# One x tile loaded ahead of the weights, its transpose halved, and one K product moved, in the QKV stage of a fused attention and feed-forward kernel

## The chip, the cores and the metric

The kernel runs on one core of a Trainium2 chip. The metric is the device time of one execution in microseconds (us). The span, from the first to the last instruction in the trace, comes out 2 us shorter. A few executions are in a slow state (over 1.5% above the fastest); they enter no ratio. The short names of the engines are PE (TensorE, matmuls), DVE (VectorE), ACT (ScalarE), POOL (GpSimd) and SP (SyncE, which issues most loads).

## The reference, cut to what matters

```python
def reference(A_x, A_wqkv, A_wo, B_x, B_w_gate, B_w_up, B_w_down):
    ...
    x = A_x                                  # 1 x 2048 x 1024, bf16
    xn = _layernorm(x, axis=-1)
    s = _A_ref(xn, A_wqkv, A_wo)             # linear attention: K and V of all tokens are summed first
    g = _silu(_B_ref(xn, B_w_gate, B_w_up, B_w_down))
    return x + s * g
```

Only the first 45 us of the program are changed. In them, 16 tiles of 128 tokens are normalised and transposed, and are multiplied with the K and V columns of `wqkv`. Those columns form four chunks of 512, and chunks 0 and 1 are K. The products of each tile are then summed into a state (`kvz`).

## The kernel before

The loads in program order. SP issues nearly all of them on its one queue; ACT issues half of x tile 0:

```python
        def load_x(i):
            if i == 0 and D % 2 == 0:
                h = D // 2
                x_loads[i] = nc.sync.dma_start(out=x_ap(i)[:, 0:h], in_=x2[0:P, 0:h])
                nc.scalar.dma_start(out=x_ap(i)[:, h:D], in_=x2[0:P, h:D])
                return
            x_loads[i] = nc.sync.dma_start(out=x_ap(i), in_=x2[i * P:(i + 1) * P, :])
        # ... (load_wkv(c) loads chunk c of the K and V weights, 1 MB)
        load_x(0)
        load_wkv(0, halves=2 if DC % 2 == 0 else 1)
        nx = 1
        for c in range(1, NCH):
            if nx < NT:
                load_x(nx)
                nx += 1
            load_wkv(c)
        for i in range(nx, NT):
            load_x(i)
        for wt, wv in ((wq_sb, wqkv_v), (wo_sb, wo_v)):
            for c in range(NCC):
                nc.sync.dma_start(out=wt[:, :, c * CW:(c + 1) * CW], in_=wv[:, :, c * CW:(c + 1) * CW])
```

The steps are `emit_stats` and `emit_rstd` (layer norm statistics), `emit_N` (normalise, on DVE), `emit_TR` (eight PE transposes into PSUM, then a copy to `xnT`), `emit_Bmm(i, c)` (product of tile i with chunk c, eight matmuls), `emit_Bev(i, c)` (its evacuation by ACT and DVE) and `emit_C(i)` (accumulation of tile i into `kvz`). Each engine runs its own instructions in the order written here:

```python
        emit_stats(0); emit_rstd_act(0); emit_N(0); emit_TR(0)      # (one call per line in the source)
        emit_stats(1); emit_rstd_act(1); emit_N(1)
        emit_Bmm(0, 0)
        emit_TR(1)
        ln_pre(2, nc.vector)          # statistics and rstd of tile 2, all on DVE
        emit_Bev(0, 0)
        emit_Bmm(0, 1)
        emit_N(2)
        emit_Bmm(1, 0)
        # ...
```

## Time and profile before

| | before |
|---|---|
| first three executions | 767.11, 766.46, 768.77 us |
| span of the profiled execution | 767.3 us (that execution took 769.27 us) |
| PE busy | 754.1 us (98%) |
| PE's longest wait | 2.35 us, for the rows of tile 1 |
| half-clock stretch | 3.41 us, from 12.22 us |

The page of before: span, busy time with instruction counts, and the chain that ended last by engine.

```profile
span 767.3 us, 10482 instructions
PE 754.1 (98%) x3717; PEld 349.6 (46%) x3717; DVE 551.5 (72%) x1076; ACT 345.8 (45%) x473; POOL 287.4 (37%) x413
PE 92%; DVE 4%; ACT 1%; DMA 1%; issue 1%; SPq 0%; ACTq 0%; DVEq 0%
```

PE is the limit, so the gaps in its timeline are what can be won. The timeline of before, PE alone; columns are start, duration, engine, line, operation, count, and in brackets the idle time before it and what ended it.

```profile
6.19 0.72 PE L470 MATMUL tr_ps<-ident,xn 128*128 128x128 bf16 x8 [0.24 <-DVE xn L443]
7.11 1.04 PE L486 MATMUL kv_ps<-wkv_sb,xnT 128*128 128x512 bf16 x4 [0.20 <-DVE xnT L473]
8.34 1.02 PE L486 MATMUL kv_ps<-wkv_sb,xnT 128*128 128x512 bf16 x4 [0.19 <-DMA wkv_sb<-in_A_wqkv_dram]
11.71 0.62 PE L470 MATMUL tr_ps<-ident,xn 128*128 128x128 bf16 x8 [2.35 <-DVE xn L443]
12.17 10.48 PE L486 MATMUL kv_ps<-wkv_sb,xnT 128*128 128x512 bf16 x40
```

PE finishes the first product at 9.36 and idles until 11.71. The chain of waits says for what; columns are start, duration and piece.

```profile
2.21 6.79 DMA xp<-in_A_x_dram
...
9.02 1.29 DVE stats L405 x2
...
11.11 0.56 DVE xn L443
...
11.71 0.62 PE tr_ps L470 x8
```

The load of x tile 1, issued at 2.21, lands at 9.00, and 2.71 us of statistics and normalising follow. The view of DMA issues, narrowed to 2.7 to 2.9 us, shows the next load in the queue, chunk 1; the last number is the time to landing.

```profile
wkv_sb<-in_A_wqkv_dram SPq DMA_DIRECT2D x1, 1024.0 KB, 9.2
```

Issued at 2.75, it lands at 11.98, only 0.19 us before PE uses it. Last, the windows view of before: busy time of each engine in a stretch, then granted clock, DMA busy share and GB/s.

```profile
5.00:6.00 1.00, 0.95 (x4) 0.17 (x2) 0.54 (x3) 0.29 (x1) 0.00 (x0) 1.00 0.84 267
6.00:7.00 1.00, 0.72 (x8) 0.45 (x8) 0.83 (x4) 0.00 (x0) 0.00 (x0) 1.00 0.93 293
8.80:12.22 3.42, 1.07 (x12) 0.57 (x11) 2.20 (x5) 1.61 (x3) 0.00 (x0) 1.00 1.08 376
12.34:15.76 3.42, 3.42 (x9) 1.22 (x8) 3.11 (x11) 0.94 (x2) 0.00 (x0) 0.52 1.09 356
```

The third line is the stretch that holds the gap, with PE busy 1.07 of 3.42 us. In the fourth the clock is half (0.52): nine matmuls in 3.42 us.

### The profile page before, as it was taken

How to read it: one execution, taken by the hardware profiler on the slowest of the kernel's cores; microseconds unless marked ns; L12 is line 12 of the kernel's file. 1: busy time of each engine (PE TensorE's matmuls, PEld its weight loads, DVE VectorE, ACT ScalarE, POOL GpSimd, SP SyncE). 2: the span in 40 equal slices, each digit the busy share in tenths (PEclk: the TensorE clock that was granted, in tenths of full speed). 3: DMA queues.
4: the chain of work that ended last, by engine and by line, in shares of the span. 5: the costliest groups of instructions: out<-in, count | busy, mean ns of one | idle time of the engine just before them, and what ended most of it. 6: DMA issues, size and time to landing. Idle time of an engine off the chain costs nothing.

```text
span 767.3 us, 10482 instructions
## 1 busy us (share of the span) xinstructions
PE 754.1 (98%) x3717; PEld 349.6 (46%) x3717; DVE 551.5 (72%) x1076; ACT 345.8 (45%) x473; POOL 287.4 (37%) x413
## 2 busy tenths in 40 slices
PE   7999999999999999999999999999999999999996
PEld 3544444444444444444444444444444444444443
DVE  6788557997666588878889885358676776787335
ACT  3545667788853566566447411132323223201111
POOL 0477499959685255858656000110000000200000
PEclk9999999999999999999999999999999999999999
DMA  9945868769889769898888227399654444530923
GB/s 308 352 95 114 229 221 274 248 222 259 237 304 262 256 228 312 283 333 298 308 309 290 89 81 262 113 356 334 229 185 167 165 169 175 187 114 23 296 73 117
DMA packets 105396, 170.29 MB, mean 222 GB/s; under 512 B 34688, under 2 KB 82176, under 8 KB 94720
## 3 DMA queue, kind: packets, MB, share of 16 engines
q1 hardware_dynamic: 94960, 121.00, 50.3%
q0 software_dynamic: 7936, 44.31, 15.0%
q10 hardware_dynamic: 2448, 4.33, 1.6%
q8 instruction: 29, 0.48, 0.3%
q14 instruction: 23, 0.19, 0.1%
HBM read 111.67 MB, written 50.59 MB: 211 GB/s over the span
## 4 chain that ended last, share of the span: by engine, by line
PE 92%; DVE 4%; ACT 1%; DMA 1%; issue 1%; SPq 0%; ACTq 0%; DVEq 0%
PE zw L725 25%; PE kv_ps L486 14%; PE dzw L910 13%; PE xb L725 12%; PE s_ps L659 7%; PE yb L725 6%; PE dx L910 6%; PE q_ps L170 4%; PE dy L910 3%; PE kvz L508 1%; DMA xp<-in_A_x_dram 1%; DVE o_blk L640 1%; PE nd_ps L632 1%; DVE pqT L141 1%; DVE pqT L153 0%
## 5 line engine op out<-in xcount | busy, mean ns | idle before, releaser
L725 PEld LDWEIGHTS <-w_sb 128*128 128x128 f16 (+1 forms) x1568 | 152.2, 98 | 184.3 <-issue 1.7
L725 PE MATMUL xb<-xnT,w_sb 128*128 128x512 bf16 x448 | 115.0, 379 | 1.1 <-ACT sg L800 1.1
L486 PE MATMUL kv_ps<-wkv_sb,xnT 128*128 128x512 bf16 x512 | 115.5, 383 | 0.4 <-DVE xnT L473 0.2
L725 PE MATMUL zw<-xnT,w_sb 128*128 128x512 bf16 x448 | 105.8, 379 | 0.0
L725 PE MATMUL zw<-S,w_sb 128*128 128x512 f16 x448 | 105.8, 379 | 0.0
L280 POOL TENSOR_TENSOR w_sb<-w_sb 128x512 f16<-128x512 bf16 x42 | 48.9, 1165 | 96.7 <-DVE w_sb L268 36.3
L247 ACT ACTIVATE w_sb<-w_sb 128x2048 bf16<-128x2048 bf16 x42 | 79.9, 1902 | 9.1 <-DMA w_sb<-in_B_w_up_dram 7.1
L910 PE MATMUL dx<-w_sb,hT 128*128 128x512 bf16 x224 | 82.8, 379 | 0.0
L486 PEld LDWEIGHTS <-xnT 128*128 128x128 bf16 x512 | 49.0, 98 | 57.2 <-issue 2.4
L910 PEld LDWEIGHTS <-hT 128*128 128x128 bf16 (+1 forms) x448 | 43.8, 98 | 52.9
L910 PE MATMUL dzw<-w_sb,hT 128*128 128x512 f16 (+1 forms) x224 | 64.4, 379 | 0.0
L170 PE MATMUL q_ps<-xnT,wq_sb 128*128 128x512 bf16 x256 | 58.2, 379 | 0.0
L753 DVE SCALAR_TENSOR_TENSOR s<-yb,rc_all,s 128x512 f32<-128x512 f32 x42 | 31.5, 749 | 37.0 <-ACT s L752 37.0
L659 PE MATMUL s_ps<-wo_sb,oT 128*128 128x512 bf16 x256 | 57.8, 379 | 0.0
L725 PE MATMUL yb<-S,w_sb 128*128 128x512 f16 x224 | 57.4, 379 | 0.0
L801 ACT ACTIVATE sg<-cg 128x1024 bf16<-128x1024 f32 x28 | 29.6, 1057 | 56.6 <-DVE cg L794 56.6
L794 DVE SCALAR_TENSOR_TENSOR cg<-zw,rc_all,s 128x1024 f32<-128x1024 f32 x28 | 35.9, 1283 | 25.4 <-PE zw L725 14.0
L850 POOL TENSOR_TENSOR hs<-hT 128x512 f16<-128x512 bf16 x2 | 2.5, 1258 | 132.6 <-ACT sg L801 132.6
L281 POOL TENSOR_TENSOR w_sb<-w_sb 128x512 f16<-128x512 bf16 x42 | 50.1, 1193 | 3.3
L283 POOL TENSOR_TENSOR w_sb<-w_sb 128x512 f16<-128x512 bf16 x42 | 50.8, 1210 | 0.0
L282 POOL TENSOR_TENSOR w_sb<-w_sb 128x512 f16<-128x512 bf16 x42 | 49.8, 1186 | 0.0
L884 POOL DMA_DIRECT2D out_dram<-io x16 | 8.7, 542 | 101.9 <-DVE io L883 101.6
(148 smaller groups left out, 1099.3 us busy)
## 6 DMA issues: line engine op xcount, KB each, us to landing
w_sb<-pk_g SPq DMA_DIRECT2D x27, 1024.0 KB, 6.0
pk_g<-w_sb POOLq DMA_DIRECT2D x14, 1024.0 KB, 5.4
pk_u<-w_sb POOLq DMA_DIRECT2D x14, 1024.0 KB, 6.4
w_sb<-wd SPq DMA_DIRECT2D x14, 1024.0 KB, 5.0
w_sb<-pk_u SPq DMA_DIRECT2D x14, 1024.0 KB, 4.9
w_sb<-wd SPq DMA_DIRECT2D x14, 768.0 KB, 5.8
w_sb<-in_B_w_gate_dram SPq DMA_DIRECT2D x14, 512.0 KB, 5.3
w_sb<-in_B_w_down_dram SPq DMA_DIRECT2D x28, 256.0 KB, 4.5
```

Of the source, the lines that this page charges most:

```text
L170: nc.tensor.matmul(q_ps[:], lhsT=wq_sb[:, dc, g * P:(g + 1) * P], rhs=xn_ap(dc, btok), start=(dc == 0), stop=(dc == DC - 1))
L247: nc.scalar.activation(out=junk, in_=raw_view(key, t), func=ACT.Square, accum_out=asum[:])
L280: nc.gpsimd.tensor_tensor(out=T1, in0=b12, in1=b11, op=ALU.subtract)
L281: nc.gpsimd.tensor_tensor(out=T2, in0=b22, in1=T1, op=ALU.subtract)
L282: nc.gpsimd.tensor_tensor(out=T3, in0=b22, in1=b12, op=ALU.subtract)
L283: nc.gpsimd.tensor_tensor(out=T4, in0=b21, in1=T2, op=ALU.subtract)
L486: mm = nc.tensor.matmul(kv_ps[:], lhsT=xn_ap(dc, tok), rhs=wkv_sb[:, dc, c * CW:(c + 1) * CW], start=(dc == 0), stop=(dc == DC - 1))
L659: mm = nc.tensor.matmul(s_ps[:], lhsT=oT[:, c, ttok], rhs=wo_sb[:, c, cc * CW:(cc + 1) * CW], start=(c == 0), stop=(c == G - 1))
L725: mm = nc.tensor.matmul(out, lhsT=lhs(k), rhs=rhs(k), start=(first and k == 0), stop=(k == HK - 1), skip_group_check=True)
L753: nc.vector.scalar_tensor_tensor(out=s2[:], in0=y_[:], scalar=rc, in1=s1[:], op0=ALU.mult, op1=ALU.add)
L794: nc.vector.scalar_tensor_tensor(out=d12, in0=zw[:], scalar=rc, in1=s2[:, None, :].to_broadcast([P, 2, TB]), op0=ALU.mult, op1=ALU.add)
L910: nc.tensor.matmul(out, lhsT=lhs, rhs=rhs, start=first, stop=lastk, skip_group_check=True)
```

## The change

The intent: start x tile 1 right away on the ACT queue instead of behind 1 MB of weights; transpose it in two halves that are copied by two engines (for this, tile 0's copies move from DVE to ACT); and transpose tile 2 and do its first K product earlier, so that PE has work while weights are on their way.

```diff
@@ load_x
+            if i == 1:
+                x_loads[i] = nc.scalar.dma_start(out=x_ap(i), in_=x2[i * P:(i + 1) * P, :])
+                return
@@ order of the loads
         load_x(0)
+        load_x(1)
         load_wkv(0, halves=2 if DC % 2 == 0 else 1)
-        nx = 1
+        nx = 2
         for c in range(1, NCH):
+            load_wkv(c)
             if nx < NT:
                 load_x(nx)
                 nx += 1
-            load_wkv(c)
@@ emit_N
-            if i == 0:
+            if i < 2:
@@ emit_TR
-            nh = 2 if i == 0 else 1
+            nh = 2 if i < 2 else 1
 ...
-                if i < 2:
+                if i == 1 and hh == 0:
                     nc.vector.tensor_copy(out=dst, in_=tr_ps[:])
                 else:
                     nc.scalar.copy(out=dst, in_=tr_ps[:])
@@ order of the stage
         emit_Bmm(0, 2)
+        emit_TR(2)
         emit_Bev(1, 1)
 ...
         ln_pre(4)
-        emit_TR(2)
+        emit_Bmm(2, 0)
         emit_Bmm(0, 3)
 ...
-                emit_Bmm(i, c)
+                if (i, c) != (2, 0):
+                    emit_Bmm(i, c)
```

## The prediction

> **What bounds the kernel now.** The tensor engine (PE). The page gives it 98% of the 767.3 us span, and PE matmuls fill 92% of the chain that ended last. By the table of waits all its waits come to about 7 us, and the largest, 2.4 us, is the one this change aims at: the timeline shows PE finishing the first K product at 9.36, idle until 11.71, when tile 1's normalised rows arrive (chain of waits: x tile 1 issued 2.21, landed 9.00, statistics, rstd, normalise, transpose). After 12.17 PE is gap-free until about 131 us, so whatever is gained or lost near 12 to 30 us should reach the end of the kernel unchanged. In the stretch 12.3 to 15.8 the granted clock was 0.52 (matmul starts 0.43 us apart instead of 0.22), costing about 1.7 us more. The Trainium skill, "TensorE: Matmul & The Clock Gate", Part 1, describes that: a free-running 3.4 us window with too little PE work halves the clock for the next one. The trace agrees: one half-clock stretch of 3.41 us, after a window with PE busy 1.06 of 3.41 us.
>
> **What the change does.** x tile 1 goes to the ACT queue, beside weight chunk 0 instead of behind it. The skill, "DMA: Bandwidth & Descriptors", section "Issuing engines are not separate DMA queues", says queues interleave on the same 16 engines, so this reorders bytes and adds no bandwidth. Estimate from the windows view (about 0.35 MB per us): x1 lands near 5.5; the second half of weight chunk 0 slips by 0.26 MB / 0.36 = 0.7 us, from 8.3 to 9.0. Statistics of tile 1 then follow tile 0 directly (6.5), normalised rows at about 9.3. The first K product ends near 10.1 (0.7 later), transposes of tile 1 follow at once.
>
> **Why most of the 2.4 us isn't won.** The next product in PE order needs weight chunk 1. The DMA view shows it issued at 2.75 and landing 9.2 us later: 11.95, only 0.2 us before PE used it. The bytes ahead of it (x0, x1, chunks 0 and 1) are unchanged, so it still lands near 11.9. The wait changes its name, from x1 to weight chunk 1, and PE gains 0.2 to 0.3 us there.
>
> **Clock.** PE work in the window before 12 us rises from 31% to about 50 to 55%, as the late half of the first product, the transposes and the wait are spread more evenly. If that keeps the full clock, up to 1.7 us is regained, but not all: at full clock the PE meets VectorE's chain for tile 2 (x2 lands 12.7; rstd by small operations until 17.2; first K evacuation 18.4; normalise 18.9), which frees PSUM and feeds transpose 2. I count 0.5 to 0.8 us of new waits.
>
> **The other parts.** Both copies of tile 0's transpose move to ScalarE (1.02 us for 1024 columns there, 0.69 on VectorE): 0.1 to 0.2 us later start, hidden by the chunk-0 wait. Transpose 2 earlier puts its ScalarE copy (1.02 us) before the evacuation of K product (1,1), whose bank product (2,0) needs: 0.4 to 0.6 us wait. Moving (2,0) adds no work.
>
> **Sum.** With the clock kept: 1.2 to 1.5 us faster than a half-clock run; with half clock again: 0.3 faster to 0.3 slower. Predicted 766.2 us, range 764.6 to 768.0; faster by over 2%: 0.005, within 2%: 0.99, slower: 0.005.
>
> **Right if:** x1 lands before 6.5; PE waits 1 us or more for weight chunk 1, ending at 11.6 to 12.0; transposes of tile 1 end before 11; the span changes by less than 2 us. **Wrong if:** weight chunk 1 lands before 11 (gain 2 to 3 us), or the reordered ScalarE work stalls PE by over 1 us near 20 to 24 us.

## More of the kernel before

Tiles 0 to 3 are transposed on PE. From tile 4 on, `emit_N` ends with a DMA transpose on the SP queue:

```python
            if i >= NPE:              # NPE = 4
                xn_tiles.pop(i)
                nc.sync.dma_start_transpose(out=xn_ap(slice(0, DC), slice(i * P, (i + 1) * P)), in_=xn[:])
```

## The result, and the profile after

| | before | after |
|---|---|---|
| median of four | 767.8 us | 765.94 us |
| lowest and highest | 766.46, 768.77 | 765.63, 766.43 |
| span of the profiled execution | 767.3 us | 764.2 us |

The ratio is 0.9978, with a 95% interval of 0.9959 to 0.9996, so "same" at the 2% mark. All ratios here are the mean time of one kernel's fast runs over that of the other's fast runs of the same rounds, so not quite the ratio of the medians. The two profiled executions differ by 3.1 us, more than the 1.9 us of the medians: that of before, at 769.27 us, was slower than all four in the table. That is the first sign that one pair of profiles isn't the whole story.

The page of after, span and chain:

```profile
span 764.2 us, 10485 instructions
PE 89%; DVE 6%; DMA 2%; ACT 1%; issue 1%; POOL 1%; SPq 0%; DVEq 0%; ACTq 0%
```

PE's timeline of after:

```profile
6.98 1.90 PE L490 MATMUL kv_ps<-wkv_sb,xnT 128*128 128x512 bf16 x8 [0.35 <-ACT xnT L479]
8.72 0.65 PE L474 MATMUL tr_ps<-ident,xn 128*128 128x128 bf16 x8
10.12 7.07 PE L490 MATMUL kv_ps<-wkv_sb,xnT 128*128 128x512 bf16 x32 [0.76 <-DMA wkv_sb<-in_A_wqkv_dram]
17.02 0.61 PE L474 MATMUL tr_ps<-ident,xn 128*128 128x128 bf16 x8
17.51 1.89 PE L490 MATMUL kv_ps<-wkv_sb,xnT 128*128 128x512 bf16 x8
19.72 5.34 PE L490 MATMUL kv_ps<-wkv_sb,xnT 128*128 128x512 bf16 x24 [0.33 <-ACT r_t L151]
...
40.01 1.90 PE L490 MATMUL kv_ps<-wkv_sb,xnT 128*128 128x512 bf16 x8 [1.03 <-DMA xnT<-xn]
```

The transposes of tile 1 now follow the first product at once. The 2.35 us wait for tile 1 has become a wait of 0.76 us for chunk 1, then one of 0.33 us for an evacuation. At 40 us there is a wait that before did not have, 1.03 us for a DMA transpose. The chain of waits of after leads to it:

```profile
31.42 0.55 DVE xn L447
32.00 7.97 DMA xnT<-xn
40.01 1.90 PE kv_ps L490 x8
```

The DMA transpose of tile 4, issued at 32.00, takes 8.0 us to land. The windows view of after, for the same four purposes as before:

```profile
5.00:6.00 1.00, 0.71 (x5) 0.20 (x4) 0.73 (x3) 0.20 (x1) 0.00 (x0) 1.00 1.09 383
6.00:7.00 1.00, 0.65 (x9) 0.38 (x9) 1.00 (x3) 0.66 (x2) 0.00 (x0) 1.00 1.11 352
8.13:11.55 3.42, 2.66 (x19) 1.39 (x18) 1.93 (x6) 2.12 (x3) 0.00 (x0) 1.00 1.09 355
12.34:15.76 3.42, 3.42 (x18) 1.53 (x17) 2.89 (x17) 1.02 (x3) 0.00 (x0) 1.00 1.09 356
```

PE is busy 2.66 of 3.42 us before 12 us, and the clock stays full: 18 matmuls instead of 9 in the last window. The surprise is in the first two lines. The DMA engines now move 383 and 352 GB/s where before they moved 267 and 293. Chunk 1 lands at 10.08 instead of 11.98, although the same bytes stand ahead of it.

To follow PE's lead, I use two marks from the traces: the start of the accumulation of tile 2 (A2) and of tile 3 (A3). The texts call them the third and the fourth accumulation; the first experiment of the second batch calls A3 "the third tile's last accumulation". In before they are at 36.39 and 43.76 us, in after at 33.17 and 41.75. So the lead is 3.2 us at A2 and 2.0 us at A3, and it is 3.1 us at the end. The timeline of before around its two marks:

```profile
36.39 0.62 PE L508 MATMUL kvz<-v_sb,pk_sb 128*128 128x129 bf16 x8
36.85 7.07 PE L486 MATMUL kv_ps<-wkv_sb,xnT 128*128 128x512 bf16 x32
43.76 0.62 PE L508 MATMUL kvz<-v_sb,pk_sb 128*128 128x129 bf16 x8
```

The last eight of the 32 matmuls are the first product of tile 4, because each accumulation comes after the next tile's first product. It starts at 42.03, only 0.77 us after the DMA transpose that it needs has landed (41.26).

The lead grows again at 335 us, where before waits 1.1 us for an ACT result (its load of `w_up` landed late) and after does not.

### The profile page after: what moved, and what is told of

Read it like the earlier page. It is cut to its first block, busy times and chain, and to the rows that moved or that the text cites. A ratio compares the mean times of both kernels' runs of the same rounds, so it can differ in the third digit from the quotient of the medians.

```text
span 764.2 us, 10485 instructions
## 1 busy us (share of the span) xinstructions
PE 752.2 (98%) x3717; PEld 349.2 (46%) x3717; DVE 551.0 (72%) x1075; ACT 346.8 (45%) x476; POOL 287.5 (38%) x413
## 4 chain that ended last, share of the span: by engine, by line
PE 89%; DVE 6%; DMA 2%; ACT 1%; issue 1%; POOL 1%; SPq 0%; DVEq 0%; ACTq 0%
PE zw L731 25%; PE dzw L916 13%; PE xb L731 12%; PE kv_ps L490 11%; PE s_ps L665 7%; PE yb L731 6%; PE dx L916 6%; PE q_ps L170 4%; PE dy L916 3%; DMA xp<-in_A_x_dram 1%; DMA xnT<-xn 1%; PE kvz L512 1%; DVE o_blk L646 1%; PE nd_ps L638 1%; DVE pqT L141 1%
## 5 line engine op out<-in xcount | busy, mean ns | idle before, releaser
L490 PE MATMUL kv_ps<-wkv_sb,xnT 128*128 128x512 bf16 x512 | 113.8, 379 | 2.5 <-DMA xnT<-xn 1.0
L247 ACT ACTIVATE w_sb<-w_sb 128x2048 bf16<-128x2048 bf16 x42 | 79.9, 1902 | 10.1 <-DMA w_sb<-in_B_w_up_dram 7.3
```

The lines of the kernel that those rows point to most:

```text
L247: nc.scalar.activation(out=junk, in_=raw_view(key, t), func=ACT.Square, accum_out=asum[:])
L490: mm = nc.tensor.matmul(kv_ps[:], lhsT=xn_ap(dc, tok), rhs=wkv_sb[:, dc, c * CW:(c + 1) * CW], start=(dc == 0), stop=(dc == DC - 1))
```

## The experiments

All kernels gave correct results. Each call timed its kernels against before on one chip, so there are 46 executions of before by now, from 765.60 to 769.75 us, in five groups.

Three theories. **S**: the stall for x tile 1, the late chunk 1 and the half clock happen in every execution of before. **R**: they belong to some executions. **F** (a floor, formed after the first batch): what is won before 40 us is given back at tile 4's DMA transpose.

### First batch: which part, and does it repeat?

**A copy of before**, no edit.

> A copy of the kernel before, to see what of its first profile repeats. Theory S (the stall is systematic: with x tile 1 behind weight chunk 0 on one queue, some of the 16 DMA engines fall up to 2 us behind each time): weight chunk 1 lands at 11.5 us or later again, spread over 2 us across the 16 engines, the K product of tile 1 starts at 12.1 or later, and a half-clock stretch follows. Theory R (that spread was an accident of one execution): chunk 1 lands near 10.1 to 10.5 with under 0.5 us of spread, x tile 1 lands near 7.5, PE waits for it about 1 us instead of 2.4, and no half-clock stretch follows; the span is then 764.5 to 765.5 instead of 767.3. The times of before are in two groups so far (766.5 to 767.1 and 768.5 to 768.8), which favours R happening in part of the runs.

Measured: 765.63 to 770.67 us over six executions, and before beside it 765.60 to 768.73 over eleven. The lowest are as fast as the change ever was. In the profile x tile 1 landed at 7.96 and chunk 1 at 10.92, its 16 engines 1.1 us apart. PE still waited 2.06 us, and the half clock followed. The windows view of this copy:

```profile
8.26:11.68 3.42, 1.36 (x13) 0.76 (x12) 2.27 (x6) 2.10 (x4) 0.00 (x0) 1.00 1.09 364
11.68:15.09 3.41, 3.41 (x10) 1.22 (x8) 3.06 (x13) 1.40 (x4) 0.00 (x0) 0.50 1.09 356
```

So neither theory holds as written: the wait and the half clock repeat, the landings vary by a microsecond, and R holds for the time. A2 was at 35.36, 1.0 us earlier than in the first profile of before. The profiled execution, the slowest of the six at 770.67 us, also waited 1.1 us at 335 us, and a second half-clock stretch followed at 335.94, so its time says little about the start.

**Only the load moved**: the first two parts of the diff, without halves and without the moved product.

```diff
+            if i == 1:
+                x_loads[i] = nc.scalar.dma_start(out=x_ap(i), in_=x2[i * P:(i + 1) * P, :])
+                return
 ...
         load_x(0)
+        load_x(1)
```

> Only the x tile 1 load is moved (ACT queue, ahead of the weights); transposes and K product order as before. If the load is what pays: weight chunk 1 lands near 10.1, PE resumes there, no half-clock stretch, and the time is within 0.5 us of the whole change (765.5 to 766.4). If the halves and the moved product carry the gain: within 0.5 us of before (767 to 768).

Measured: 765.62 to 768.02, median 766.00; chunk 1 at 10.61; no half clock; PE waited 1.0 us for tile 1, now because DVE still has tile 0's copies ahead of its statistics. It is as fast as the whole change, as the load theory expected. But it is not faster than before on that chip (ratio 1.000, 0.998 to 1.002).

**Filler**: before with six dummy matmuls in the gap.

```diff
         emit_Bmm(0, 0)
+        wps2 = psC.tile([P, CW], FP32, name="fill_ps", tag="C")
+        for k in range(6):
+            nc.tensor.matmul(wps2[:], lhsT=warm[:, 0:P], rhs=warm[:], start=True, stop=True)
         emit_TR(1)
```

> The kernel before with six dummy matmuls (1.3 us at full clock) put in PE's gap before the transposes of tile 1; loads unchanged. It measures the clock by itself. If the half clock is worth its 1.7 us: no half-clock stretch in 12 to 16 us, though PE still waits for x tile 1; the third tile's transposes start up to 1 us earlier than in before (at most, since VectorE's chain for tile 2 ends at the same time), and the time falls 0.5 to 1.2 us against before in runs that had the half clock. If the clock is a side issue: same time as before within 0.3 us.

Measured: no half clock. From the start of tile 1's transposes to A2 it took 23.61 us (11.65 to 35.26); in before and in its copy it took 24.68 (11.71 to 36.39, 10.68 to 35.36). So the half clock costs 1.07 us, at the upper end of what was expected. Less than the nominal 1.7 us: at full clock PE waits 0.45 us for an evacuation that it doesn't wait for at half clock. In the times it doesn't show: 765.84 to 767.37, ratio 1.0005 (0.999 to 1.002), so the expected 0.5 to 1.2 us were missed.

**The change without its load**: the first two parts of the diff undone.

```diff
-            if i == 1:
-                x_loads[i] = nc.scalar.dma_start(out=x_ap(i), in_=x2[i * P:(i + 1) * P, :])
-                return
 ...
-        load_x(1)
```

> The change without its load: x tile 1 stays behind weight chunk 0; tile 1's transposes in halves and the moved K product stay. If the load is what pays: no faster than before, 766.8 to 768.5, with a PE wait of 1 to 2.4 us for tile 1's rows. If the reordering pays by itself: within 0.5 us of the whole change.

Measured: four fast executions of 765.87 to 766.31 and one slow of 781.83. This counts as a miss: it was not slower than the whole change. In its profile x tile 1 happened to land early (7.22), chunk 1 too (10.21). A2 was at 33.42, and then PE waited 0.9 us for the DMA transpose of tile 4; A3 was at 41.81.

This was the hint. Four profiles with A2 at 33.2 to 33.9 (after, its copy below, the load alone, and this one) all have A3 at 41.75 to 41.91.

### Second batch: is there a floor?

**A copy of the change**, no edit.

> A copy of the whole change, timed beside before on one chip. So far its gain is 3.1 us by the two first profiles, 1.7 us by the first four times, and nothing by the lowest times (before 765.6, change 765.6). Theory F (floor): PE's early lead is given back at about 40 us, where the first product of tile 4 waits for a DMA transpose that is queued behind the wq and wo loads; before mostly reaches that floor too, and only its bad executions (half clock after 12 us, late loads near 330 us) are slower. F expects the lowest times of both within 0.2 us of each other, the change under 1 us faster in the mean, a PE wait of about 1 us for the DMA transpose near 39 to 40 us in this profile, and the third tile's last accumulation starting near 41.8 us. Rival G (the gain is a plain 1.5 to 3 us in every execution): lowest times differ by 1.5 us or more.

Measured: fast executions 765.77 to 766.19 (one slow, 778.75), before beside it 765.79 to 768.92, ratio 0.9991 (0.9977 to 1.0004). The lowest times are 0.02 us apart, the wait at 39.2 us is 0.93 us, and A3 is at 41.90. F's numbers hold; a plain gain in every execution (G) is refuted. All eight fast executions of the change lie at or below 766.43; 15 of the 46 of before do.

**The change with late wq and wo loads.**

```diff
-        for wt, wv in ((wq_sb, wqkv_v), (wo_sb, wo_v)):
-            for c in range(NCC):
-                nc.sync.dma_start(out=wt[:, :, c * CW:(c + 1) * CW], in_=wv[:, :, c * CW:(c + 1) * CW])
 ...
                 if c == 3 and i in (4, 6, 7):
                     prep(1)
+                if c == 3 and i == 5:
+                    for wt, wv in ((wq_sb, wqkv_v), (wo_sb, wo_v)):
+                        for cc in range(NCC):
+                            nc.sync.dma_start(out=wt[:, :, cc * CW:(cc + 1) * CW], in_=wv[:, :, cc * CW:(cc + 1) * CW])
```

> The whole change, with the wq and wo loads (not needed before 130 and 166 us) issued after tile 5 instead of right after the x tiles. F expects: the DMA transpose of tile 4 lands by 36 us instead of 40, no PE wait near 40 us, everything after it 1.0 us earlier, span near 763.1 and lowest time near 764.6, under the lowest of both kernels. If another limit lies right behind, the wait at 40 us is gone but the span is no shorter than 763.7.

Measured: the DMA transpose landed at 35.76, the wait at 40 us was gone, A3 was at 41.15. Lowest 764.82, ratio 0.9980 (0.9967 to 0.9994). The profile itself fell in the slow state (a span of 789.7, from waits after 217 us). F holds.

**Before with late wq and wo loads** (the same edit).

> The kernel before with the same late wq and wo loads. Its PE comes to tile 4 at 40 to 42 us by itself, so F expects 0 to 0.5 us of gain: lowest time 765.2 to 765.6. The difference of this one to the change with late loads is what the change is worth with the floor taken away: F expects 0.7 to 2 us, in a profile without a half-clock stretch 0.7 to 1.3 us. G expects the same difference as with the floor.

Measured: 765.93 to 767.57, ratio 1.0002 (0.9989 to 1.0015), so the floor is not what holds before. The lowest time missed the expected 765.2 to 765.6. The lowest times of the two kernels with late loads differ by 1.1 us, and their A3 by 1.2 us (42.36 and 41.15), as F expected. This profile also settles when the half clock strikes. PE waited 2.15 us, as long as in the copy of before, and yet no half clock followed:

```profile
6.91:10.32 3.41, 2.13 (x12) 0.75 (x9) 2.19 (x5) 0.07 (x1) 0.00 (x0) 1.00 1.06 359
10.32:13.74 3.42, 2.36 (x17) 1.35 (x18) 2.41 (x5) 2.59 (x4) 0.00 (x0) 1.00 1.10 358
```

The windows here follow the 3.41 us grid that the trace's clock record shows for this execution. The grid has another phase in each execution. Here its border at 10.32 cuts the gap in two, and both windows are busy over 60%.

**Only the load, with late wq and wo loads** (the two edits above).

> Only the x tile 1 load moved, plus the late wq and wo loads: tells what the halves and the moved K product are worth once the floor is gone. In the two profiles with the floor, PE was at the last product of tile 2 at 33.9 us with the load alone and at 33.2 us with the whole change, so about 0.7 us slower than the whole change with late loads is expected: lowest time near 765.2. If the halves and the moved product are worth nothing, the same as the whole change with late loads within 0.2 us.

Measured: lowest 764.78, ratio 0.9985 (0.9972 to 0.9999), A3 at 40.88. The expected 0.7 us did not come: the halves and the moved product are worth nothing that these runs show. PE's timeline of this kernel tells why:

```profile
9.91 0.62 PE L471 MATMUL tr_ps<-ident,xn 128*128 128x128 bf16 x8 [0.97 <-DVE xn L444]
10.46 7.07 PE L487 MATMUL kv_ps<-wkv_sb,xnT 128*128 128x512 bf16 x32
...
40.88 0.62 PE L509 MATMUL kvz<-v_sb,pk_sb 128*128 128x129 bf16 x8
```

Tile 1's rows come a microsecond later than in the whole change, but the next product starts at 10.46, and chunk 1 had landed only at 10.41.

And here is the floor itself. The view of DMA issues, narrowed to the DMA transpose of tile 4, first of after:

```profile
xnT<-xn SPq DMA_TRANSPOSE x1, 8.0
```

then of before:

```profile
xnT<-xn SPq DMA_TRANSPOSE x1, 7.0
```

then of the kernel with only the load and late wq and wo loads:

```profile
xnT<-xn SPq DMA_TRANSPOSE x1, 3.1
```

In all seven traces with early wq and wo loads this transpose lands 0.9 us after the last wo load, whenever it was issued: at 39.96 after 39.03 in after, at 41.26 after 40.34 in before.

### Third batch: what holds PE between 10 and 33 us?

**Swap**: the change with late loads, and PE does tile 1 with chunk 0 before tile 0 with chunk 1.

```diff
-        emit_Bmm(0, 1)
+        emit_Bmm(1, 0)
         emit_N(2)
-        emit_Bmm(1, 0)
+        emit_Bmm(0, 1)
```

> The whole change with late wq and wo loads, and PE does tile 1 with weight chunk 0 before tile 0 with chunk 1, so nothing waits for chunk 1 until about 11 us. In the traces so far PE waits 0.7 to 1.2 us for chunk 1 there. Theory C (chunk 1 is what PE is held to): the wait at 9.5 to 10.5 us goes and the fourth accumulation starts about 0.7 us earlier than the 41.15 us of the unswapped one, lowest time near 764.2. Theory V (right behind it VectorE's chain for tile 2, from its landing at 10.8 us, holds PE): the wait goes, but the waits at 17 to 21 us grow by as much (from 0.3 to about 1 us) and the accumulation starts within 0.3 us of 41.15. I expect V.

Measured: V's way. The wait for chunk 1 is gone and a new one on DVE's chain has come, as the view of waits of this kernel, up to 45 us, shows; columns are total us, times, longest.

```profile
PE tr_ps L471 <- DVE xn L444: 0.6, 2, 0.4
```

The 0.4 us are at 17.3, before the transposes of tile 2. A3 is at 41.24, within 0.1 us of the unswapped one, though chunk 1 landed 0.3 us later. Four executions of 764.62 to 765.27, ratio 0.9969 (0.9947 to 0.9991).

**x tile 1 from SP, still ahead of the weights**, with late loads:

```diff
-                x_loads[i] = nc.scalar.dma_start(out=x_ap(i), in_=x2[i * P:(i + 1) * P, :])
+                x_loads[i] = nc.sync.dma_start(out=x_ap(i), in_=x2[i * P:(i + 1) * P, :])
```

> The whole change with late wq and wo loads, but x tile 1 is issued from SP like before, only ahead of the weights: tells the order of the bytes from the second queue. If order is all: x tile 1 lands near 4.5 us, weight chunk 1 at 10.1 to 10.7, and the time equals the whole change with late loads (lowest 764.8) within 0.2 us. If the second queue matters (the five runs with x tile 1 behind chunk 0 on SP had chunk 1 landing at 10.2 to 12.0, the five with it on ACT at 10.1 to 10.7): chunk 1 lands later than 10.9, with its 16 engines over 1 us apart, and the time is up to 0.7 us longer.

Measured: x tile 1 landed at 4.35, but chunk 1 only at 12.13, its engines 2.0 us apart, so the second theory's numbers. Two executions were slow (its profile too), the fast ones took 769.78 and 770.53, a ratio of 1.004 (1.001 to 1.007) to before. That is 5 us above the kernel that it was compared with (lowest times), and the late chunk 1 explains 1.4 to 1.8 us of it (A3 at 42.59 instead of 41.15 and 40.80). The rest I can't explain; the slow profile waits 11.8 us for DMA transposes of the attention output after 217 us, and whether the fast executions do is not known.

**A repeat of the change with late loads**, no further edit.

> A repeat of the whole change with late wq and wo loads, whose first profile fell in the slow state: no wait near 40 us, fourth accumulation at about 41.1 us, span near 763.0, lowest time near 764.8, and faster than before by 1 to 2.5 us in the mean of the fast runs.

Measured: A3 at 40.80, no wait near 40 us, lowest 764.84: as expected. The mean was not: 764.84 to 768.76 and one slow, ratio 0.9992 (0.9971 to 1.0014). The execution of 768.76 is the profiled one, and the view of waits of this kernel shows a wait at 217 us, which a half-clock stretch followed:

```profile
PE s_ps L666 <- ACT s_sb L669: 2.1, 1, 2.1
```

So late loads lower the floor by about 1 us, but on this chip the kernel was not reliably faster.

**x tile 2 before chunk 1**, in the swapped kernel:

```diff
         load_wkv(0, halves=2 if DC % 2 == 0 else 1)
-        nx = 2
+        load_x(2)
+        nx = 3
```

> Theory X, formed from the twelve traces: what holds PE from 10 to 33 us is neither x tile 1 nor weight chunk 1 but the landing of x tile 2, through VectorE's statistics and rstd for it, the evacuation queued behind them and the PSUM bank that this frees. The third accumulation (kvz) starts 22.4 us (22.2 with the swap) after x tile 2 lands in all seven traces of the whole change, 22.65 where x tile 1 comes behind chunk 0, 23.7 with the half clock. This kernel is the swapped one with late wq and wo loads, and x tile 2 loaded before weight chunk 1 (chunk 1 then lands 0.7 us later, which the swap hides). Theory X: x tile 2 lands near 8.2 us instead of 11.0 to 11.7; PE runs nearly without waits from 9.5 us (0 to 0.7 us in all to 33 us); the third accumulation starts at 32.0 to 32.9 us instead of 33.2 to 33.9, more than 23.8 us after x tile 2 landed; lowest time 763.6 to 764.3. If chunk 1 is the limit instead: the third accumulation is no earlier than 33.4 us, and the lowest time 764.6 or more.

Measured: x tile 2 landed at 8.93 and chunk 1 at 11.92, both later than expected. A2 was at 33.55, not 32.0 to 32.9, so theory X falls as a statement about what holds PE alone, although the lowest time, 764.27, lies in the range that X gave. The constant that had suggested it (A2 22.4 us after x tile 2) broke, 24.6 here. But x tile 2 always landed 0.7 us after chunk 1 in those traces, so the constant could not tell the two apart. What PE waits for here, from the view of waits of this kernel:

```profile
PE kv_ps L488 <- ACT xnT L477: 0.5, 1, 0.5
PE kv_ps L488 <- ACT r_t L151: 0.4, 1, 0.4
PE kv_ps L488 <- DVE xnT L475: 0.3, 1, 0.3
```

The view leaves out idle times under 0.15 us, and two short waits for weights hide there: by the starts of its matmuls PE loses 0.11 us until chunk 1 lands (11.92) and 0.24 us until chunk 2 lands (15.61). So what is left are short waits of several kinds, none over 0.5 us in the view, and PE is near its own work. Six executions of 764.27 to 766.33, median 764.50; ratio 0.9965 (0.9948 to 0.9981). This and the swapped kernel have lowest times about 1 us or more below those of the kernels before and after. I did not time them in the same rounds as the change.

### The account

The traces record when each of the 16 engines finishes its part of a load. The table gives A2 less the landing of chunk 1 for the kernels that keep all of before's order or all of the change's. (In before's order PE waits for x tile 1, which lands 2.96 to 3.00 us ahead of chunk 1 in those four traces.)

| kernel | chunk 1 lands, first to last engine | half clock at 12 us | A2 | A2 less chunk 1 |
|---|---|---|---|---|
| before | 9.8 to 11.98 | yes | 36.39 | 24.41 |
| copy of before | 9.8 to 10.92 | yes | 35.36 | 24.44 |
| filler | 9.8 to 11.93 | no | 35.26 | 23.33 |
| before, late loads | 9.8 to 11.66 | no | 34.99 | 23.33 |
| after | 9.9 to 10.08 | no | 33.17 | 23.09 |
| copy of after | 10.0 to 10.34 | no | 33.43 | 23.09 |
| after, late loads | 9.9 to 10.69 | no | 33.78 | 23.09 |
| its repeat | 9.8 to 10.34 | no | 33.44 | 23.10 |
| the same, x tile 1 from SP | 10.1 to 12.13 | no | 35.23 | 23.10 |

Within one order, A2 follows the landing of chunk 1 to a few hundredths. That names the delivery as a whole and not chunk 1 alone: x tile 1 in before's order, and x tile 2 in both, land at nearly fixed distances from it. The change itself takes 0.24 us off (23.33 to 23.09), and in executions where before meets the half clock another 1.1. The rest of the 3.22 us at A2 between the first two profiles, 1.90 us, is the earlier delivery (chunk 1 at 10.08 instead of 11.98). That the profiles of one and the same kernel differ there by 1.06 us (11.98 and 10.92) shows that much of it is chance. About 1.0 of the 1.90 us may belong to the change: that is the difference of the mean landings with x tile 1 on ACT's and on SP's queue (last section).

## Why the prediction was right or wrong, point by point

The time, 765.94 against 766.2 predicted, and the class were right, in part by luck: an early delivery that was not predicted (1.9 us at A2) and a loss that was not predicted (1.2 us before A3) worked in opposite directions. Of the marks under "Right if", two held (x1 at 5.55, transposes of tile 1 done at 9.37) and two failed: PE waited 0.76 us for chunk 1, ending at 10.12, and the span changed by 3.1 us. The first mark under "Wrong if", chunk 1 before 11, came true.

- **"PE gains 0.2 to 0.3 us there"**, and **"The wait changes its name, from x1 to weight chunk 1"**: right. The account gives 0.24 us. The wait for chunk 1 is there in after (0.76 us), in its copy (0.7 us), and in both other traces of that order with late loads.
- **"x1 lands near 5.5"** and transposes of tile 1 before 11: right (5.55; 9.37).
- **The clock**: right that PE's window gets busier (78%, more than the 50 to 55% predicted) and the full clock is kept. It was wrong to take the half clock as a property of before. It depends on where the execution's 3.41 us grid lies (Trainium skill, "TensorE: Matmul & The Clock Gate", Part 1, which calls the window free-running; the traces agree: of the three profiles with a gap of over 2 us, two have a half-clock stretch).
- **"it still lands near 11.9"**, and the second half of chunk 0 at 9.0: wrong (10.08 and 7.09), and not for this execution alone: in all seven traces with x tile 1 on ACT's queue and chunk 1 right behind the same bytes it landed at 11.01 or earlier. I took the landing of one execution for the bandwidth. It was the slowest of 16 engines, the first of which had finished at 9.8 (Trainium skill, "DMA: Bandwidth & Descriptors", section "Why a DMA increments its semaphore by 16 and not by 1": the engines finish independently. The trace of before agrees: 9.8 to 12.0). By my own text a chunk 1 before 11 would have meant 2 to 3 us of gain, and at A2 it was 3.2.
- **"whatever is gained or lost near 12 to 30 us should reach the end of the kernel unchanged"**: the step that failed outright. PE had no gap near 40 us in before because it came there late. The DMA transpose of tile 4 landed at 41.26, and PE needed it at 42.03, so the slack was 0.77 us. In after it landed 1.30 us earlier, at 39.96. So a lead of at most 0.77 + 1.30 = 2.07 us could pass; PE came with 3.2 us, waited 1.03 us and kept 2.0 us at A3. That the wait comes from the wq and wo loads ahead is shown by the late loads that took it away.
- **"I count 0.5 to 0.8 us of new waits"**, and **"0.4 to 0.6 us wait"** for the evacuation behind transpose 2's copy: the mechanism is there, as one wait in both roles, 0.33 us in the view. By the starts of the matmuls it cost 0.49 us (0.70 us between two starts instead of 0.22). So the second size fits and the first was too large, and they are not two waits.
- **"1.2 to 1.5 us faster than a half-clock run"**: mis-sized as profiles go (3.1 us between the two). At equal delivery the account gives 0.24 + 1.1 = 1.3 us at A2, inside that range. The delivery added 1.9 us, in part luck, the transpose of tile 4 took 1.2 us back, and the wait at 335 us, which I did not foresee, added 1.1 us. What makes that load of `w_up` late stays open.

What the change does, then: it makes the early stage robust. Before seems to need an early x tile 1 and a lucky clock window in order to reach the floor at tile 4. That is inferred from the traces of its variants and from its times, as no trace of one of before's quickest executions was kept. After reached the floor in both of its traces, and all eight fast times lie within 0.8 us. It does not lower the floor.

## What to carry to other kernels

A wait that is removed at the head of a queue hands the engine to the next thing in that queue, so write down when each later load lands before counting the gain. An engine without gaps downstream proves only that its inputs came in time for its present pace: look at the landing of each input, and at what stands ahead of it in its queue, for the slack that is left. For gains of one or two microseconds compare many executions and marks inside the trace, not one pair of profiles.

## What the Trainium skill lacked or had wrong

- "TensorE: Matmul & The Clock Gate", Part 1, gives the rule that idle gaps of PE should stay below about 3.4 us, and no busy share. Here idle times of 2.35 and 2.06 us in one window were enough: windows with PE busy 31% and 40% (1.07 of 3.42 us, 1.36 of 3.42), and later in the copy of before 47% (1.59 of 3.41 us from 332.53), were followed by half clock, and the others that I measured, with 62% and more (2.13 of 3.41), were not. All traces cut on their own grids add 49% (1.67 of 3.42 us from 235.84, in the slow profile of x tile 1 from SP), which was not followed either.
- The same page, section "Terms", puts the cost of throttled time at that time multiplied by the missing share of the clock, so an estimate of 1.7 us for 3.41 us at half clock. Here the net cost was 1.07 us, since at full clock PE meets a later wait of 0.45 us.
- "DMA: Bandwidth & Descriptors", section "Issuing engines are not separate DMA queues", says that a second issuing engine only saves issue time. Here chunk 1 landed at 10.2 to 12.1 us (mean 11.5) in six traces with x tile 1 on SP's queue, and at 10.1 to 11.0 (mean 10.5) in seven with it on ACT's, the bytes ahead being the same. The first engine finished at 9.7 to 10.2 in all of them; the laggards differ. Six against seven traces on several chips, and x tile 2 ahead of chunk 1, with x tile 1 on ACT's queue, had chunk 1 at 11.92, so it is a tendency, and its cause stays open.
- No page says how long a DMA transpose takes behind bulk loads on the same queue. It took 7.0 and 8.0 us to land behind the wq and wo loads and 3.1 us without them.
